# Keys of the last two batches transposed by DMA, their block sums added on GpSimd and VectorE, and u transposed from SBUF to SBUF

## The chip, the cores and the metric

The kernel runs on one NeuronCore of a Trainium2 chip, in one launch. The metric is the device time of one execution in microseconds (us). Three runs of the kernel before gave 272.8, 274.03 and 274.05 us; the median is 274.03. A further execution was taken with the hardware profiler: it took 272.19 us, of which 270.40 us are the span that the profile shows, from the first instruction to the last.

In the profile PE is TensorE (PEld its weight loads), DVE is VectorE, ACT is ScalarE, POOL is GpSimd and SP is SyncE. SPq is the queue of DMA issues on SP. L359 is line 359 of the kernel before.

## The reference

The input is q, k and v of shape (4 batches, 8 heads, 768 positions, 64). First comes a block-sparse attention, then a two-layer mixer on its output x of shape (4, 768, 512):

```python
k_rep = k.reshape(B, H, 12, 64, D).mean(axis=3)          # one mean key per block of 64
gate_scores = einsum('bhsd,bhnd->bhsn', q, k_rep)        # blocks of the future: -1e9
sel = top-3 blocks of gate_scores, and the own block     # per query
scores = q @ k.T / 8, where the block is selected and j <= i, else -1e9
attn_out = softmax(scores) @ v
...
xt = x.transpose(0, 2, 1)
h = maximum(xt @ w_tok1, 0) @ w_tok2
u = x + h.transpose(0, 2, 1)
out = u + maximum(u @ w_ch1, 0) @ w_ch2
```

So each head needs K transposed (for the scores) and the sums of K over blocks of 64 (for the gate), and each batch needs u and u transposed (for `u @ w_ch1`).

## The kernel before

The attention works on 16 pairs of heads, four to a batch. For a pair, the two heads lie side by side: K and Q are loaded as fp32 tiles of 128 positions by 6 blocks by 128 columns (`load_qk`, L265, two DMAs each, with rows of 256 bytes). TensorE transposes them in six 128x128 fp32 steps (`transposes`, L359) into PSUM; ScalarE copies the result to SBUF (`evac_t`, L368, tiles kt and qt); GpSimd casts it to fp16, one cast for each head, into KA and Q (`cast`, L374). VectorE sums kt over blocks (`ksum`, L382) and puts the sums in place (`kcopy`, L390). Then come the gate (five fp32 matmuls, L400), the top three on VectorE, a mask that is transposed on TensorE (L443) and copied into spare rows of Q (L451), the scores (three groups a head, L465), the exponentials on ScalarE (L478), the causal cut on VectorE (L485), the product with V (21 matmuls a head, L496), and the division by the row sums, which writes x16 (L515). V is loaded by one DMA a pair and cast on GpSimd (`cast_v`, L280).

For each batch the token mixer (`tok1` L527 and `umix` L539; for batch 0 in column parts, L558 and L572) gives u in fp16, 128 positions by 6 blocks by 512 columns (L547, L581). In batch 0, TensorE transposes u (L589) and VectorE copies it to uT (L597). In batches 1 to 3, SP stores u to DRAM (`store_u`, L344) and a DMA transpose reads it back into uT (`turn_u`, L350). The channel mixer is `ch1` (L608; for each of 12 groups of 128 hidden columns, 4 matmuls over 512 positions and 4 over 256), a ReLU on ScalarE (L618) or VectorE (L620), `ch2` (L629, 12 matmuls a block of 128 positions), an addition of u on VectorE (L637) and the output's store on SP (L641).

Nothing is ordered at run time. Every step is an `Op` with an engine, a cost in nanoseconds that its author wrote down, its dependences and a priority; `plan` places them one by one and gives each engine a fixed order, in which the instructions are then issued. An engine that waits for one instruction holds all that stand behind it. The pairs follow each other; the mixers of a finished batch fill the gaps. Tiles come from rings of fixed size (`RINGS`): two PSUM tiles `big` for scores and transposes, three PSUM banks, two kt tiles, three output tiles ob, and so on. A tile is handed out again once its last user is done.

The code holds a second way for K, for the pairs i >= VIA; with VIA = 16 no pair takes it. There, `load_k8` (L290) loads K of both heads as 96 partitions by 2 heads by 8 positions by 64 columns, in the ring of kt; `cast_k8` (L311) casts it into K16, a tile whose other columns hold zeros (`k16_zero`, L325) and block indicators (`k16_ind`, L329); `store_k` (L318) writes K16 to DRAM and `turn_k` (L322) transposes it by DMA from DRAM straight into KA; `ksum8` (L298) sums the 8 positions of each partition and `ksum_pe` (L305), one fp32 matmul with a 96x12 indicator, sums partitions to blocks.

Of the kernel before, what the change touches and what calls it, by code (L numbers as in the profile page):

```python
# [10 lines left out]
F16 = mybir.dt.float16  # L11
AF = mybir.ActivationFunctionType
ALU = mybir.AluOpType
AX = mybir.AxisListType
# [15 lines left out]
FIRST = 4  # L30
TRI = 1
EARLY = 1
VIA = 16
UVIA = 1
LEAD = 960.0
WARM, COLD, WARM_END = 120, 20, 17000.0
# [141 lines left out]
def kernel(  # L178
# [11 lines left out]
    nc = tc.nc  # L190
    B, H, S, D = q.shape
    NB = S // 64
    NJ = S // 128
    DM = H * D
    DT = moe_w_tok1.shape[1]
    DC = moe_w_ch1.shape[1]
    NCC = DM // 128
# [7 lines left out]
    dram = ctx.enter_context(tc.tile_pool(name="dr", bufs=1, space=bass.MemoryType.DRAM))  # L205
# [11 lines left out]
    def sb(tag, shape, dt, name):  # L217
        return sp.tile(shape, dt, tag=tag, bufs=RINGS[tag], name=name)

    def ps(tag, shape, name, dt=FP):  # L220
        if tag == "big":
            return pp.tile([128, 1024], FP, tag=tag, bufs=RINGS[tag], name=name)
        return pp.tile(shape, dt, tag=tag, bufs=RINGS[tag], name=name)
# [16 lines left out]
    T = {}  # L240
    ops = []

    def op(eng, occ, rec, deps, prio, fn, takes=(), size=0):
        o = Op(eng, occ, rec, deps, prio, fn, takes, size)
        ops.append(o)
        return o

    def pe(occ, deps, prio, fn, takes=(), tail=170):
        return op("PE", occ, occ + tail, deps, prio, fn, takes)
# [4 lines left out]
    def dve(occ, deps, prio, fn, takes=()):  # L254
        return op("DVE", occ, occ + 84, deps, prio, fn, takes)
# [12 lines left out]
    def load_v(i):  # L268
        b, h = pairs[i]

        def f():
            t = sb("v32", [128, 2, NJ, D], FP, f"v32_{i}")
            T["v32", i] = t
            nc.sync.dma_start(out=t.rearrange("p g j d -> p (g j) d"),
                              in_=v[b, h:h + 2].rearrange("g (j p) d -> p (g j) d", p=128))
        return f
# [7 lines left out]
    def load_k8(i):  # L284
        b, h = pairs[i]

        def f():
            t = sb("kt", [128, 2, 8, D], FP, f"k8_{i}")[0:96]
            T["k8", i] = t
            nc.sync.dma_start(out=t.rearrange("p g t d -> p g (t d)"),  # L290
                              in_=k[b, h:h + 2].rearrange("g (p t) d -> p g (t d)", t=8))
        return f

    def ksum8(i):
        def f():
            t = sp.tile([96, 2, D], FP, tag="kp", bufs=2, name=f"kp_{i}")
            T["kp", i] = t
            nc.vector.tensor_reduce(out=t, in_=T["k8", i].rearrange("p g t d -> p g d t"), axis=AX.X, op=ALU.add)  # L298
        return f

    def ksum_pe(i):
        def f():
            p = ps("bank", [128, NB], "kps")
            T["kst", i] = p
            nc.tensor.matmul(out=p, lhsT=T["kp", i].rearrange("p g d -> p (g d)"), rhs=blk, start=True, stop=True)  # L305
        return f

    def cast_k8(i):
        def f():
            y = i % 2  # L310
            nc.gpsimd.tensor_copy(out=K16[y].rearrange("p t (g c) -> p g t c", g=4)[:, 0:4:3, :, :], in_=T["k8", i])  # L311
        return f

    def store_k(i):
        def f():
            t = dram.tile([S, 256], F16, tag=f"ks{i % 2}", name=f"kscr_{i}")
            T["kscr", i] = t
            nc.sync.dma_start(out=t.rearrange("(p t) c -> p (t c)", t=8), in_=K16[i % 2].rearrange("p t c -> p (t c)"))  # L318
        return f

    def turn_k(i):
        return lambda: nc.sync.dma_start_transpose(out=KAX[:, i % R, :, :], in_=T["kscr", i])  # L322

    def k16_zero(y):
        return lambda: nc.gpsimd.memset(K16[y].bitcast(FP), 0.0)  # L325

    def k16_ind(y):
        def f():
            for c in (64, 128):  # L329
                nc.gpsimd.tensor_copy(out=K16[y][:, :, c:c + NB],  # L330
                                      in_=blk.rearrange("p (o n) -> p o n", o=1).broadcast_to([96, 8, NB]))
        return f

    def zero_q(r):
        def f():
            nc.gpsimd.memset(QA[r][0][64:128, :].bitcast(FP), 0.0)
            nc.gpsimd.memset(QA[r][1][0:64, :].bitcast(FP), 0.0)
        return f

    def store_u(b):  # L340
        def f():
            t = dram.tile([S, DM], F16, tag=f"us{b % 2}", name=f"uscr_{b}")
            T["uscr", b] = t
            nc.sync.dma_start(out=t.rearrange("(j p) c -> p j c", p=128), in_=T["u", b])  # L344
        return f

    def turn_u(b):
        def f():
            T["uT", b] = sb("uT", [128, NCC, S], F16, f"uT_{b}")
            nc.sync.dma_start_transpose(out=T["uT", b], in_=T["uscr", b])  # L350
        return f

    def transposes(t32, i):
# [31 lines left out]
    def kcopy(i):  # L385
        def f():
            kst = T["kst", i]
            r = i % R
            for lo, c in ((64, 0), (0, NB)):
                nc.vector.tensor_reduce(out=ks2[r][lo:lo + 64, c:c + NB],  # L390
                                        in_=kst[lo:lo + 64, :].rearrange("p (n o) -> p n o", o=1),
                                        axis=AX.X, op=ALU.add)
        return f
# [199 lines left out]
    def uput(b, cc):  # L593
        def f():
            if cc == 0:
                T["uT", b] = sb("uT", [128, NCC, S], F16, f"uT_{b}")
            nc.vector.tensor_copy(out=T["uT", b][:, cc, :], in_=T["utps", b, cc])  # L597
        return f

    CH = ((0, 512), (512, 768))  # L600
# [1 line left out]
    def ch1(b, fc, n):  # L602
        def f():
            a, e = CH[n]
            p = ps("bank", [128, e - a], "c1")
            T["c1", b, fc, n] = p
            for cc in range(NCC):
                nc.tensor.matmul(out=p, lhsT=wc1_16[:, cc, 128 * fc:128 * fc + 128],  # L608
                                 rhs=T["uT", b][:, cc, a:e], start=(cc == 0), stop=(cc == NCC - 1))
        return f  # L610

    def relu2(b, fc, n):
# [38 lines left out]
    O = {}  # L651
# [16 lines left out]
    for i in range(NP):  # L668
        b, h = pairs[i]
        base = 10.0 * i  # L670
        pre = 10.0 * (i - (AHEAD if i < FIRST else LATER))
        old = i - R

        def last_scores(x):
            return [O.get(("sc", old, x, g)) for g in range(3)]

        if i >= VIA:
            kb = Buf("kt")
            ld = op("SP", 500, 0, [], pre - 12, load_k8(i), [kb], size=1400)
            O["ksum", i] = dve(1100, [ld], pre + 1, ksum8(i))  # L680
            nb = Buf("bank")
            O["kpe", i] = pe(115, [O["ksum", i]], pre + 1, ksum_pe(i), [nb])
            O["kcopy", i] = dve(260, [O["kpe", i], O.get(("gate", old))], pre + 1, kcopy(i))
            nb.users.append(O["kcopy", i])
            y = i % 2
            if i < VIA + 2:
                O["kz", y] = op("POOL", 1100, 1150, [], pre - 1, k16_zero(y))
                O["ki", y] = op("POOL", 400, 450, [O["kz", y]], pre - 1, k16_ind(y))
            O["castk", i] = op("POOL", 1150, 1200, [ld, O["ki", y], O.get(("kst", i - 2))], pre + 3, cast_k8(i))
            kb.users += [O["ksum", i], O["castk", i]]  # L690
            O["kst", i] = op("SPO", 600, 0, [O["castk", i], O.get(("cast", "kt", i, 0))], pre + 3.1, store_k(i), size=1600)
            O["kturn", i] = op("SPO", 600, 0, [O["kst", i]] + last_scores(0) + last_scores(1), pre + 3.2, turn_k(i), size=2500)
            O["cast", "kt", i, 0] = O["cast", "kt", i, 1] = O["kturn", i]
        zq = [op("POOL", 880, 930, [], pre - 1, zero_q(i))] if 0 < i < R else []
        for t32, src, off in (("kl", k, 0), ("ql", q, 0.1))[i >= VIA:]:
            bf = Buf(t32)
# [4 lines left out]
            name = "kt" if t32 == "kl" else "qt"  # L701
            tb = Buf(name)
# [19 lines left out]
        ld = op("SP", 500, 0, [], pre + 2, load_v(i), [vb], size=1700)  # L722
# [47 lines left out]
    for b in range(B):  # L770
        fill = 1000.0 * (b + 1)
        mix = fill - LEAD if b else fill
        early = -1.0
        norms = [O["norm", i, x] for i in range(4 * b, 4 * b + 4) for x in range(2)]
        hb = Buf("h1")
        ub = Buf("u")
        if b == 0:
# [13 lines left out]
            uadds = [[O["uadd", b, c, n] for n in range(2)] for c in range(4)]  # L791
        else:
# [12 lines left out]
            uadds = [[O["uadd", b, j] for j in range(NJ)]] * NCC  # L805
        tb = Buf("uT")
        if b >= UVIA:
            O["ust", b] = op("SPO", 600, 0, uadds[0], early, store_u(b), size=3000)
            O["uturn", b] = op("SPO", 600, 0, [O["ust", b]], early, turn_u(b), [tb], size=3500)
            ub.users.append(O["ust", b])  # L810
        for cc in range(NCC if b < UVIA else 0):
            bk = Buf("bank")
            O["utr", b, cc] = pe(336, uadds[cc], mix + (cc + 0.6 if b == 0 else 10 + cc), utr(b, cc), [bk])
# [16 lines left out]
        for j in range(NJ):  # L830
            cuts = ((0, DM),) if b < B - 1 or j < NJ - 1 else ((0, 320), (320, DM))
            for lo, hi in cuts:
# [11 lines left out]
                s = op("SPO", 600, 0, [o], early, store(b, j, lo, hi), size=2 * (hi - lo))  # L844
# [76 lines left out]
```

## Time and profile before

| | |
|---|---|
| median of three runs | 274.03 us |
| profiled execution | 272.19 us, span 270.40 |
| six K transposes of a pair on PE, L359 | 96 instructions in all 16 pairs |
| evacuation of K on ACT, L368 | 16, 799 ns each |
| casts of K on POOL, L374 | 32, 845 ns each |
| sums of K on DVE, L382 | 15 of 942 ns and one of 957 |
| weight loads issued on POOL, L663 and L665 | 8, 384 KB each |
| store of u, L344, issue to landing | 3.7 to 7.7 us |
| DMA transpose of u, L350 | three, 3.5 to 4.3 us on SPq, 5.6 to 7.7 to landing |

A group of the profile shows the line, the engine, the operation, what it writes and reads, the shapes, the count, then the busy time, the mean of one in ns, and the idle time of the engine before it with what ended it. The time of one matmul includes its latency; matmuls overlap, so what one costs is read from the start of one to the start of the next. The slices cut the span into 40 parts of 6.76 us; a digit is the busy share in tenths.

### The profile page before, as it was taken

To read this page: it belongs to the slowest core of one execution; us is meant where nothing else is said; L and a number is where in the kernel's file an instruction comes from. 1 tells how busy PE (TensorE), PEld (TensorE's weight loads), DVE (VectorE), ACT (ScalarE), POOL (GpSimd) and SP (SyncE) were. 2 spreads that over 40 slices of the span, in tenths; PEclk is the share of its full clock that TensorE was granted. 3 is DMA by queue.
4 is the path that set the end of the run, shared out by engine and by line. 5 is a ranking of instruction groups with operands and counts; after the bars stand their busy time and mean duration, and the time that the engine had idled before them with its cause. 6 is when DMAs were issued, how large, how long until landed. Compare 5 with 4: busy or idle time off the path is not lost.

```text
span 270.4 us, 5927 instructions
## 1 busy us (share of the span) xinstructions
PE 262.6 (97%) x2309; PEld 174.5 (65%) x2309; DVE 161.0 (60%) x561; ACT 142.6 (53%) x188; POOL 81.5 (30%) x112
## 2 busy tenths in 40 slices
PE   8899999999999999999999999999999999999994
PEld 5787588877787877776876655544455544465443
DVE  4558968997979777879888533334233252333222
ACT  2367997777888898788487704430024400044100
POOL 8688816763465365336432000000000000000000
PEclk9999999999999999999999999999999999999999
DMA  8999999999999985480741121003920017510032
GB/s 173 205 212 224 189 215 214 197 200 200 213 209 228 212 176 133 103 174 3 158 117 41 39 77 42 0 2 116 260 89 2 0 48 196 153 72 0 2 135 97
DMA packets 94411, 34.67 MB, mean 128 GB/s; under 512 B 85616, under 2 KB 90888, under 8 KB 94384
## 3 DMA queue, kind: packets, MB, share of 16 engines
q1 hardware_dynamic: 90272, 29.89, 50.5%
q0 software_dynamic: 3392, 4.15, 9.1%
q8 instruction: 18, 0.29, 0.5%
q10 hardware_dynamic: 720, 0.25, 0.5%
q14 instruction: 9, 0.07, 0.1%
HBM read 27.21 MB, written 8.65 MB: 133 GB/s over the span
## 4 chain that ended last, share of the span: by engine, by line
PE 87%; DMA 4%; DVE 4%; ACT 3%; issue 1%; SPq 1%; DVEq 0%; ACTq 0%
PE c L629 23%; PE c L608 23%; PE sps L465 12%; PE aps L496 7%; PE gps L400 5%; DMA ql<-in_q_dram 4%; PE tql L359 4%; PE ups L539 3%; PE tkl L359 3%; PE tok L527 3%; ACT e L478 3%; PE bps L443 2%; PE warm L648 1%; PE tok L558 1%; DVE Q L451 1%
## 5 line engine op out<-in xcount | busy, mean ns | idle before, releaser
L478 ACT ACTIVATE e<-sps 128x1024 f16<-128x1024 f32 (+1 forms) x96 | 84.6, 918 | 16.9 <-PE sps L465 12.0
L608 PE MATMUL c<-uT,wc 128*128 128x256 f16 (+1 forms) x384 | 68.1, 326 | 0.2 <-ACT h L618 0.2
L618 ACT ACTIVATE h<-c 128x512 f16<-128x512 f32 x48 | 28.7, 598 | 69.0 <-PE c L608 61.7
L629 PE MATMUL c<-wc,h 128*128 128x512 f16 (+2 forms) x300 | 64.9, 370 | 0.0
L608 PEld LDWEIGHTS <-wc 128*128 128x128 f16 x384 | 37.1, 98 | 24.5 <-issue 0.4
L465 PE MATMUL sps<-Q,KA 128*128 128x512 f16 (+3 forms) x256 | 50.1, 305 | 1.0 <-ACT e L478 0.7
L629 PEld LDWEIGHTS <-h 128*128 128x128 f16 x300 | 28.8, 98 | 31.3 <-issue 0.6
L620 DVE TENSOR_SCALAR h<-c 128x256 f16<-128x256 f32 x48 | 20.2, 420 | 33.8 <-PE c L608 33.8
L637 DVE TENSOR_TENSOR ob<-u,c 128x512 f32<-128x512 f16 (+2 forms) x25 | 16.6, 666 | 38.4 <-PE c L629 38.4
L485 DVE TENSOR_TENSOR e<-e,m 128x256 f16<-128x256 f16 x90 | 31.1, 353 | 12.9 <-ACT e L478 12.2
L374 POOL CAST KA<-kt 64x768 f16<-64x768 f32 x32 | 27.0, 845 | 27.4 <-ACT kt L368 24.2
L465 PEld LDWEIGHTS <-KA 128*128 128x128 f16 x256 | 22.4, 100 | 15.2 <-issue 1.2
L374 POOL CAST Q<-qt 64x768 f16<-64x768 f32 x32 | 26.9, 841 | 10.8 <-ACT qt L368 9.3
L496 PE MATMUL aps<-V,e 128*128 128x65 f16 x672 | 27.0, 193 | 0.1
L496 PEld LDWEIGHTS <-e 128*128 128x128 f16 x672 | 25.6, 98 | 2.2 <-issue 0.4
L400 PEld LDWEIGHTS gps<-ks,qt 128*128 128x128 f32 x160 | 19.2, 192 | 2.4 <-DVE ks L390 1.3
L280 POOL CAST V<-v 128x768 f16<-128x768 f32 x16 | 13.3, 832 | 24.0 <-DMA v<-in_v_dram 19.8
L400 PE MATMUL gps<-ks,qt 128*128 128x24 f32 x160 | 20.0, 267 | 0.3 <-DVE ks L390 0.2
L368 ACT COPY kt<-tkl 128x768 f32<-128x768 f32 x16 | 12.8, 799 | 11.7 <-PE tkl L359 5.9
L515 DVE TENSOR_TENSOR x<-aps,rc 128x384 f16<-128x384 f32 x32 | 17.6, 550 | 0.5
L451 DVE COPY Q<-bps 12x640 f16<-12x640 f16 x32 | 15.5, 484 | 1.9 <-PE bps L443 0.8
L368 ACT COPY qt<-tql 128x768 f32<-128x768 f32 x16 | 12.8, 798 | 6.5 <-PE tql L359 5.7
(55 smaller groups left out, 218.0 us busy)
## 6 DMA issues: line engine op xcount, KB each, us to landing
kl<-in_k_dram SPq DMA_DIRECT2D x32, 192.0 KB, 4.8
ql<-in_q_dram SPq DMA_DIRECT2D x32, 192.0 KB, 4.6
v<-in_v_dram SPq DMA_DIRECT2D x16, 384.0 KB, 5.4
out_dram<-ob SPq DMA_DIRECT2D x23, 256.0 KB, 2.0
wc<-in_moe_w_ch_dram POOLq DMA_DIRECT2D x8, 384.0 KB, 7.4
uscr<-u SPq DMA_DIRECT2D x3, 768.0 KB, 3.7
w<-in_moe_w_tok_dram POOLq DMA_DIRECT2D x2, 384.0 KB, 6.8
out_dram<-ob SPq DMA_DIRECT2D x1, 160.0 KB, 1.8
```

Of the source, the lines that this page charges most:

```text
L359: nc.tensor.transpose(out=p[:, 128 * j:128 * j + 128], in_=t[:, j, :], identity=ident32)
L368: nc.scalar.copy(out=t, in_=p[:, 0:S])
L374: nc.gpsimd.tensor_copy(out=dst[i % R][x][lo:lo + 64, :], in_=T[name, i][lo:lo + 64, :])
L400: nc.tensor.matmul(out=g[:, j, :], lhsT=T["qt", i][:, 128 * j + 128:128 * j + 256], rhs=ks2[i % R], start=True, stop=True)
L465: nc.tensor.matmul(out=p[:, off + a:off + a + n], lhsT=KA[i % R][x][:, 128 * kk:128 * kk + 128], rhs=QA[i % R][x][:, q0 + a:q0 + a + n], s ...
L478: nc.scalar.activation(out=e[:, 0:width], in_=T["sps", i, x, g][:, 0:width], func=AF.Exp, scale=scale)
L485: nc.vector.tensor_tensor(out=d, in0=d, in1=m0, op=ALU.mult)
L496: nc.tensor.matmul(out=p[:, jq, :], lhsT=T["e", i, x, g][:, o:o + 128], rhs=V16[i % (R + 1)][:, x, kk, :], start=(kk == 0), stop=(kk == jq))
L608: nc.tensor.matmul(out=p, lhsT=wc1_16[:, cc, 128 * fc:128 * fc + 128], rhs=T["uT", b][:, cc, a:e], start=(cc == 0), stop=(cc == NCC - 1))
L618: nc.scalar.activation(out=T["h2", b][:, fc, a:e], in_=T["c1", b, fc, n], func=AF.Relu)
L620: nc.vector.tensor_scalar(out=T["h2", b][:, fc, a:e], in0=T["c1", b, fc, n], scalar1=0.0, scalar2=None, op0=ALU.max)
L629: nc.tensor.matmul(out=T["c2", b, j, lo], lhsT=T["h2", b][:, fc, 128 * j:128 * j + 128], rhs=wc2_16[:, fc, lo:hi], start=(fc == 0), stop=( ...
```

## The change

`VIA` goes from 16 to 8, so that pairs 8 to 15 (batches 2 and 3) take the second way for K. In that way the sums are made differently: the reduction over 8 positions becomes one fp32 addition on GpSimd, in place, of positions 4 to 7 onto 0 to 3 (`ksum4`, 512 elements a partition), and two on VectorE (256 and 128 elements). The cast is planned ahead of the addition, and the clearing of K16 comes after the casts of Q of pairs 5 and 6. `store_u` goes; `turn_u` reads u from SBUF and writes uT in blocks, so that uT is 6 position blocks by 4 column blocks by 128 (read by `ch1` through a rearranged view). Costs that the planner works with change with it.

```diff
-VIA = 16
+VIA = 8
...
+    def ksum4(i):
+        def f():
+            p = T["k8", i]
+            nc.gpsimd.tensor_tensor(out=p[:, :, 0:4, :], in0=p[:, :, 0:4, :], in1=p[:, :, 4:8, :], op=ALU.add)
+        return f
...
-            nc.vector.tensor_reduce(out=t, in_=T["k8", i].rearrange("p g t d -> p g d t"), axis=AX.X, op=ALU.add)
+            p = T["k8", i]
+            nc.vector.tensor_tensor(out=p[:, :, 0:2, :], in0=p[:, :, 0:2, :], in1=p[:, :, 2:4, :], op=ALU.add)
+            nc.vector.tensor_tensor(out=t, in0=p[:, :, 0, :], in1=p[:, :, 1, :], op=ALU.add)
...
-    def store_u(b):
...
-            T["uT", b] = sb("uT", [128, NCC, S], F16, f"uT_{b}")
-            nc.sync.dma_start_transpose(out=T["uT", b], in_=T["uscr", b])
+            t = sb("uT", [128, NJ, NCC, 128], F16, f"uT_{b}")
+            T["uT", b] = t.rearrange("p j c s -> p c j s")
+            nc.sync.dma_start_transpose(out=t.rearrange("p j c s -> p (j c) s"), in_=T["u", b].rearrange("p j c -> p (j c)"))
...
-                                 rhs=T["uT", b][:, cc, a:e], start=(cc == 0), stop=(cc == NCC - 1))
+                                 rhs=T["uT", b][:, cc, a // 128:e // 128, :], start=(cc == 0), stop=(cc == NCC - 1))
...
-            O["ksum", i] = dve(1100, [ld], pre + 1, ksum8(i))
+            y = i % 2
+            if i < VIA + 2:
+                O["kz", y] = op("POOL", 1000, 1050, [O["cast", "qt", 5 + y, 1]], pre - 1, k16_zero(y))
+                O["ki", y] = op("POOL", 400, 450, [O["kz", y]], pre - 1, k16_ind(y))
+            O["castk", i] = op("POOL", 1000, 1040, [ld, O["ki", y], O.get(("kst", i - 2))], pre + 3, cast_k8(i))
+            O["ksum4", i] = op("POOL", 1150, 1200, [O["castk", i]], pre + 1, ksum4(i))
+            O["ksum", i] = dve(560, [O["ksum4", i]], pre + 1, ksum8(i))
+            kb.users += [O["ksum", i]]
...
-            O["ust", b] = op("SPO", 600, 0, uadds[0], early, store_u(b), size=3000)
-            O["uturn", b] = op("SPO", 600, 0, [O["ust", b]], early, turn_u(b), [tb], size=3500)
-            ub.users.append(O["ust", b])
+            O["uturn", b] = op("SPO", 2500, 0, uadds[0], early, turn_u(b), [tb], size=3500)
+            ub.users.append(O["uturn", b])
```

More of the change, by code (lines that the diff above doesn't have):

```diff
@@ L338, in zero_q @@
         return f
-    def store_u(b):
[L341 to L345, printed above, removed]
     def turn_u(b):
         def f():
-            T["uT", b] = sb("uT", [128, NCC, S], F16, f"uT_{b}")
-            nc.sync.dma_start_transpose(out=T["uT", b], in_=T["uscr", b])
+            t = sb("uT", [128, NJ, NCC, 128], F16, f"uT_{b}")
+            T["uT", b] = t.rearrange("p j c s -> p c j s")
+            nc.sync.dma_start_transpose(out=t.rearrange("p j c s -> p (j c) s"), in_=T["u", b].rearrange("p j c -> p (j c)"))
         return f
@@ L595, in f @@
             if cc == 0:
-                T["uT", b] = sb("uT", [128, NCC, S], F16, f"uT_{b}")
-            nc.vector.tensor_copy(out=T["uT", b][:, cc, :], in_=T["utps", b, cc])
+                T["uT", b] = sb("uT", [128, NCC, NJ, 128], F16, f"uT_{b}")
+            nc.vector.tensor_copy(out=T["uT", b][:, cc].rearrange("p j s -> p (j s)"), in_=T["utps", b, cc])
         return f
@@ L684 @@
             nb.users.append(O["kcopy", i])
[L685 to L690, printed above, removed]
             O["kst", i] = op("SPO", 600, 0, [O["castk", i], O.get(("cast", "kt", i, 0))], pre + 3.1, store_k(i), size=1600)
```

## The prediction

> **What bounds the kernel now.** I read the page's busy times and slices first, then the chain of work that ended last, then the stages in which the changed code runs.
>
> ```profile
> PE 262.6 (97%) x2309; PEld 174.5 (65%) x2309; DVE 161.0 (60%) x561; ACT 142.6 (53%) x188; POOL 81.5 (30%) x112
> PE   8899999999999999999999999999999999999994
> DMA  8999999999999985480741121003920017510032
> PE 87%; DMA 4%; DVE 4%; ACT 3%; issue 1%; SPq 1%; DVEq 0%; ACTq 0%
> ```
>
> TensorE is the bound: 97% of the span, 87% of the chain, and no thin slice until the last. The DMA engines are full as well, but only for the first 14 slices (to 95 us). Busy time by stage confirms it for the stage where pairs 8 to 15 are prepared (columns: length, then busy us and instructions of PE, PEld, DVE, ACT, POOL, clock, DMA share, GB/s):
>
> ```profile
> 80.00:100.00 20.00, 20.00 (x231) 15.60 (x231) 16.40 (x69) 17.78 (x24) 10.59 (x14) 1.00 1.14 217
> 120.00:160.00 40.00, 40.00 (x420) 27.65 (x419) 31.20 (x114) 26.63 (x32) 11.97 (x14) 1.00 0.31 75
> ```
>
> PE has no idle time there. So a matmul removed is time saved, one for one, and a wait added to PE's fixed order is time lost, one for one, since no later idle time gives it back.
>
> [...] 18 warm-up matmuls at the start took 4.02 us, 223 ns each, and later ones 109 ns each (11 in 1.36 us, the last with its latency).
>
> ```profile
> 1.07 4.02 PE L648 MATMUL warm<-warm 128*128 128x256 f16 x18 [1.07 <-DVE warm L852]
> 8.47 1.36 PE L648 MATMUL warm<-warm 128*128 128x256 f16 x11
> ```
>
> **Part 1: K work on PE, eight pairs.** Removed: 6 fp32 transposes a pair. Their mean of 279 ns is latency; in the chain in order of time six take 0.66 us. Added: one fp32 matmul a pair (block sums). Nearest row: the gate, five fp32 matmuls with the same 128-column weight load in 1.08 us, 0.22 us each.
>
> ```profile
> L359 PE MATMUL tkl<-id,kl 128*128 128x128 f32 x96 | 13.6, 279 | 0.2 <-issue 0.2
> 83.80 0.67 PE tkl L359 x6
> 106.36 1.08 PE gps L400 x10
> ```
>
> Sum: 8 x 0.66 - 8 x 0.22 = 3.5 us saved, all on the path. ACT loses 8 evacuations (0.80 each, 6.4 us) and DVE 8 reductions of 942 ns against 16 adds of 256 and 128 elements (between the rows 128x120 fp32, 278 ns, and 128x512, 676 ns: about 0.42 + 0.29 = 0.71 a pair), 1.9 us less. Neither engine is the bound (17.8 and 16.4 of 20 us), so this is worth nothing by itself.
>
> **Part 2: GpSimd.** Removed: 16 casts x 0.845 = 13.5 us. Added: 8 casts of 1024 elements (832 ns for 768, so 1.1), 8 adds of 1.25, two clears of 1024 (412 ns for 384, so about 1.0) and four small copies (about 0.2): 8.8 + 10 + 2 + 0.8 = 21.6. GpSimd is busy half the time at 80 to 100 us, so the 8 us extra fit. What does not fit is one instruction that the diff doesn't show: built, the changed program has a reload of GpSimd's instruction library directly ahead of its first tensor_tensor, the add of pair 8. It sits in the middle of the program, behind a cast that waits for a load. Its place in time, from these lines of before (GpSimd, then landings of a V load issued at 54.3 and of the K halves issued from 57.4):
>
> ```profile
> 60.97 1.51 POOL L665 DMA_DIRECT2D wc<-in_moe_w_ch_dram  x2
> 64.35 0.83 POOL L280 CAST V<-v 128x768 f16<-128x768 f32 x1 [1.88 <-DMA v<-in_v_dram]
> 74.33 0.92 POOL L280 CAST V<-v 128x768 f16<-128x768 f32 x1 [2.93 <-DMA v<-in_v_dram]
> v<-in_v_dram SPq DMA_DIRECT2D x1, 384.0 KB, 9.9
> kl<-in_k_dram SPq DMA_DIRECT2D x2, 192.0 KB, 8.3
> ```
>
> Up to pair 6's V load SP's order is unchanged, so that V lands at 64.3 again. K of pair 8 is next in the queue, where the two K halves landed at 65.8 to 68.3; I take 67.2. Supply: cast 67.2 to 68.3, reload L, add 1.25, two DVE adds with their hand-over 0.85, so the block-sum matmul of pair 8 may start at 70.4 + L. Demand: PE's order in the changed program starts the channel MLP of batch 0 where it could before (59.96, held by the uT copy of L597), then runs up to that matmul: six 512-column groups x 0.86, five 256-column groups x 0.43, five scores groups of pair 5 (1.83), two aV (1.33), transposes of K 7 (0.66), 11.1 us in all: 71.1. Slack 0.7 us; the rest of L is idle PE. DVE's queue, too, stands behind the add, and kt of pair 6, whose buffer slot the K tile of pair 8 holds until its sums are made; both wait for what PE waits for already.
>
> L: from below, 0 [...]; from above 10, because the DMA engines are full here and a load that must cross them took 9.9 us to land where others in this kernel took 4.3. I take 7. Idle: 7 - 0.7 = 6.3 us. [...] Part 2 costs 6.3 + 1.7 = 8.0 us.
>
> Afterwards GpSimd's queue holds V 7, casts of K 6, cast of K 9, casts of Q 7, add of K 9: 0.83 + 1.71 + 1.1 + 1.71 + 1.25 = 6.6, plus 0.85, 7.45 us after the first add ends (76.55 at L = 7): 84.0. PE wants pair 9's sums 7.7 us after pair 8's (77.4 + 7.7 = 85.1): no second wait. With L = 0 the V load that lands at 74.3 would hold that queue, supply 81.8 against demand 78.9 and cost up to 2.9; so even a free reload leaves -0.6 to -3.5.
>
> **Part 3: K through DRAM.** A pair has two K loads of 256-byte rows less, and one load of 2 KB rows, one store and one transpose more. SP waits for the cast before each store and for the landed store before each transpose; behind stand loads of Q and V for later pairs and, near the end, output stores. Nearest row: uT, 768x512, 3.5 to 4.3 us on SP's queue and 5.6 to 7.7 to landing; K is half. Tightest is pair 8: store of pair 9 at about 80.3 (its cast), transpose behind it, landed by 88.4 even at 7.7 us; PE wants these scores 8.1 us after pair 9's sums, 93.2. Nothing is on the path: 0, at worst 2 us. If that cover went, each late transpose would cost its delay once.
>
> **Part 4: u turned from SBUF.** The store of u (3.7 to 4.6 us to landing) goes. In batch 3 it was hidden:
>
> ```profile
> 221.21 0.38 SPq L344 DMA_DIRECT2D uscr<-u  x1
> 226.57 3.53 SPq L350 DMA_TRANSPOSE uT<-uscr  x1
> 220.04 15.70 PE L629 MATMUL c<-wc,h 128*128 128x512 f16 x72
> 235.58 15.76 PE L608 MATMUL c<-uT,wc 128*128 128x512 f16 x96
> ```
>
> The turn ended near 232.2 (5.6 after issue) and its reader starts at 235.6 behind the channel MLP of batch 2. Gain 0. A transpose from SBUF is in no trace; it may take up to 14 us from 221 before it shows, twice the slowest one seen. Output stores now stand behind it on SP: with three output buffers and two outputs every 5.2 us that stands 6 us. So 0, above that up to 3 us in each of batches 2 and 3. uT is read in runs of 128 columns: no row shows such a read; 0, at worst 2 us.
>
> **Sum.** -3.5 + 8.0 + 0 + 0 = +4.5. Against the profiled execution (272.19 us: span 270.40 and 1.79 around it) 276.7. The median of the runs shown is 274.03, 1.84 above that execution; I add the change to it: 278.5.
>
> **Rivals.** *The reload is short* (0.20): PE never waits for it beyond 3 us, and the removed transposes decide: -3.5, with the late V load -0.6; about 271.8 (270.5 to 273.4). For it: no trace here shows a load, and it may be nearly free. Against: slack of 0.7 us. It decides while L is under 4.2. *Draw* (0.11): L of 4 to 6 without the clock drop, within 0.5% of 274.03. *A DMA wait besides* (0.07): SBUF transposes or K's way through DRAM come late, on top of the reload, about 285. For it: operations never seen; against: margins of 5 and more us.
>
> **Numbers.** Forecast (reload stalls PE): 0.62, own range 275.5 to 283 [...]. Range for 8 in 10: 271 to 283, from most of the short reload up to the longest stall; the bound for a difference that can be told is 0.5%, 1.4 us. Faster 0.19, same 0.12, slower 0.69.
>
> **What would show it.** A gap on PE of 5 to 9 us near 71 us, ahead of a 128x12 fp32 matmul, with GpSimd silent between a 96x1024 cast and its first tensor_tensor; PE clock below 1 after it; from there PE full and K transposes of eight pairs gone. Wrong: no such gap (then about 271), GpSimd's gap under 4 us, or PE idle ahead of scores (L465) or the channel MLP (L608) of batches 1 to 3.

## The result, and the profile after

The changed kernel took 284.35 us, the median of four runs (282.42 to 286.68), against 273.49 for the kernel before on the same chip: a ratio of 1.0375, interval [1.031, 1.0439]. The change costs about 10 us. I had forecast 278.5 and a range of 271 to 283. The size was wrong; the sign came out right by luck, since the wait that I had named, a long reload of GpSimd's library, isn't in the trace at all.

Executions of some of these versions fall into two groups that differ in how long TensorE runs at half clock; every ratio is of the faster group, while the profiles of e6 and e10 were taken in the slower one, so that the long half clock seen in them (about 13.6 us in each) is in their spans and not in their ratios.

The page of the changed kernel, busy times, slices and chain (its profiled execution took 284.52 us, span 282.7):

```profile
PE 262.3 (93%) x2277; PEld 172.0 (61%) x2277; DVE 170.3 (60%) x569; ACT 136.9 (48%) x180; POOL 89.8 (32%) x118
PE   7799999989679879999988999999999999999994
DVE  5468868965589999889698576325133262233222
PEclk9999999999999799999999999999999999999999
DMA  8999999899999779989981312000921007120032
PE 60%; DVE 16%; DMA 14%; issue 3%; POOL 3%; ACT 2%; SPq 1%; DVEq 0%; POOLq 0%
```

PE's busy time is what it was (262.6 before), but the span is 12.3 us longer, so PE now waits for 20.4 us instead of 7.8. The thin slices of PE lie between 56 and 156 us (slices of 7.07 us), where its row was full. In the chain PE falls from 87% to 60%; VectorE rises from 4% to 16%, and the DMA engines from 4% to 14%, over half of that loads of V. Most of PE's listed waits now end with VectorE. VectorE's own busy time grew by 9.3 us, where I had reckoned 1.9 less.

The stage in which the pairs of the new way are prepared and worked on, first of the kernel before, then of the changed one (columns: length, then busy us and instructions of PE, PEld, DVE, ACT, POOL, clock, DMA share, GB/s):

```profile
60.00:160.00 100.00, 99.76 (x1075) 72.68 (x1074) 80.35 (x312) 77.94 (x97) 40.74 (x50) 1.00 0.69 141
```

```profile
60.00:160.00 100.00, 88.81 (x907) 62.77 (x904) 80.16 (x286) 63.65 (x79) 46.92 (x53) 0.98 0.98 195
```

Here PE is idle for 11.2 us against 0.24. That is 11.0 of the 12.6 us by which PE's waits grew, so the experiments below are compared in this stage.

**The wait for the reload is not there.** GpSimd's timeline around its first addition:

```profile
71.02 1.04 POOL L319 CAST K<-k 96x1024 f16<-96x1024 f32 x1 [1.14 <-DMA k<-in_k_dram]
72.14 1.25 POOL L297 TENSOR_TENSOR k<-k 96x512 f32<-96x512 f32 x1
```

The cast ends at 72.06 and the addition starts at 72.14. I had put a reload of 7 us between them, which was my own estimate: no trace of before holds one. The trace here has no line of a reload, and leaves at most 0.08 us for it between the two. PE's gap ahead of pair 8's sums is 2.38 us (it starts them at 74.22). The loads of V and K make it: GpSimd waited 5.85 us for that V and began its cast at 69.05, where I had put 64.3, and the cast of K followed at 71.02 instead of 67.2.

**What VectorE does instead.** The groups of VectorE that grew or are new in the changed kernel, and L410 for comparison (busy us and mean ns of one, then idle time before it):

```profile
L434 DVE SCALAR_TENSOR_TENSOR bn<-lt,own 128x120 f16<-128x120 f32 x16 | 7.3, 456 | 0.2
L426 DVE TENSOR_TENSOR lt<-gm,m 128x120 f32<-128x120 f32 x16 | 7.3, 455 | 0.3
L305 DVE TENSOR_TENSOR k<-k 96x256 f32<-96x256 f32 x8 | 4.5, 560 | 2.9 <-POOL k L297 2.9
L306 DVE TENSOR_TENSOR kp<-k 96x128 f32<-96x128 f32 x8 | 4.5, 560 | 0.3
L410 DVE TENSOR_TENSOR gm<-gps,gbias 128x120 f32<-128x120 f32 x16 | 4.4, 277 | 6.9 <-PE gps L402 6.9
```

The two steps lt and bn, by which the top three become a mask (lt compares with the third maximum, bn makes the mask's bias of that), are the same code on the same shapes as before, where each took 278 ns. A mean of 456 hides two kinds. By line, the least, median and longest of bn before (L432) and in the changed kernel (L434) are:

```profile
L432 DVE SCALAR_TENSOR_TENSOR bn<-lt,own x16: 244/282/284, 12.4 to 146.6; 128x120 f16<-128x120 f32 x16
L434 DVE SCALAR_TENSOR_TENSOR bn<-lt,own x16: 238/280/1998, 12.5 to 164.5; 128x120 f16<-128x120 f32 x16
PEld L445: 5.4, 6
PE bps L445: 3.7, 4
```

Most are untouched, and some last up to seven times as long; TensorE's mask transposes (L445, the two lower lines: who waited for bn, us and times) then stand still. L410 did not change (its longest is 283 ns): it has the same shape as L426, but one of its inputs lies in PSUM. The long ones are those with both inputs in SBUF: the longest of L426, L434, L487, L305 and L306 are 1155, 1998, 1375, 1255 and 1237 ns, while no other group of VectorE's has one more than 20 ns above the median of its shape. When they end is the clue. GpSimd and then VectorE in the changed kernel, over the same 6 us:

```profile
86.62 1.85 POOL L376 CAST Q<-qt 64x768 f16<-64x768 f32 x2
88.53 1.04 POOL L319 CAST K<-k 96x1024 f16<-96x1024 f32 x1
90.36 1.40 POOL L297 TENSOR_TENSOR k<-k 96x512 f32<-96x512 f32 x1
```

```profile
87.70 0.90 DVE L434 SCALAR_TENSOR_TENSOR bn<-lt,own 128x120 f16<-128x120 f32 x1
88.72 0.99 DVE L487 TENSOR_TENSOR e<-e,m 128x256 f16<-128x256 f16 x1
90.74 1.16 DVE L426 TENSOR_TENSOR lt<-gm,m 128x120 f32<-128x120 f32 x1
```

Add start and duration: GpSimd's instructions end at 88.47, 89.57 and 91.76, VectorE's at 88.60, 89.71 and 91.90, each 0.13 to 0.14 us later. Each of these VectorE instructions seems to wait until GpSimd has finished the instruction in hand. The longest waited through a second one: the bn of 1998 ns runs from 144.35 to 146.35 us, past the end of an addition (145.44), and ends 0.14 us after the cast of V that follows it at once (146.21). The traces show three things: these four long instructions end 0.13 to 0.14 us after one of GpSimd's, while most keep their time (median of bn 280 ns, before 282); only those with two SBUF inputs are long; and with memsets in place of GpSimd's reads (e6 below) bn takes at most 286 ns.

Why didn't the kernel before suffer, whose GpSimd was busy for 81.5 us, most of them casts that read? GpSimd and VectorE in the kernel before:

```profile
80.29 1.77 POOL L374 CAST Q<-qt 64x768 f16<-64x768 f32 x2
87.60 1.71 POOL L374 CAST Q<-qt 64x768 f16<-64x768 f32 x2
```

```profile
82.50 0.27 DVE L424 TENSOR_TENSOR lt<-gm,m 128x120 f32<-128x120 f32 x1
91.26 0.27 DVE L424 TENSOR_TENSOR lt<-gm,m 128x120 f32<-128x120 f32 x1
```

The casts of Q are over (82.06, 89.31) before the top three reach lt. In the changed kernel the K cast and the addition stand there, and push other casts into that time too. The kernel before was not spared altogether: of its causal cuts (L485, two SBUF inputs too), whose median is 284 ns, the longest took 953; but no wait of PE for them is listed.

My theory P: GpSimd's reads hold up VectorE's two-input instructions on the way from the gate to the mask and to the block sums, and PE waits. Rivals: T, the order of the work (the K tiles share the ring of kt, so pair 6 stands behind pairs 8 and 9); C, the sums as a longer chain with late loads; U, the transposes of u from SBUF.

### The profile page after: what moved, and what is told of

It is laid out like the page before. It is cut to its first block, busy times and chain, and to the rows that moved or that the text cites. A ratio compares the mean times of both kernels' runs of the same rounds, so it can differ in the third digit from the quotient of the medians.

```text
span 282.7 us, 5873 instructions
## 1 busy us (share of the span) xinstructions
PE 262.3 (93%) x2277; PEld 172.0 (61%) x2277; DVE 170.3 (60%) x569; ACT 136.9 (48%) x180; POOL 89.8 (32%) x118
## 4 chain that ended last, share of the span: by engine, by line
PE 60%; DVE 16%; DMA 14%; issue 3%; POOL 3%; ACT 2%; SPq 1%; DVEq 0%; POOLq 0%
PE c L631 21%; PE c L610 18%; DMA v<-in_v_dram 8%; PE sps L467 5%; PE aps L498 4%; DMA ql<-in_q_dram 4%; DVE e L487 3%; PE gps L402 2%; DVE m L419 2%; PE ups L541 2%; DMA w<-in_moe_w_tok_dram 2%; PE tql L361 2%; PE tok L529 2%; DVE bn L434 2%; DVE kp L306 1%
## 5 line engine op out<-in xcount | busy, mean ns | idle before, releaser
L610 PE MATMUL c<-uT,wc 128*128 128x256 f16 (+1 forms) x384 | 66.9, 326 | 0.0
L487 DVE TENSOR_TENSOR e<-e,m 128x256 f16<-128x256 f16 x90 | 31.6, 357 | 10.3 <-ACT e L480 9.5
L467 PEld LDWEIGHTS <-KA 128*128 128x128 f16 x256 | 23.0, 101 | 15.9 <-issue 0.9
L498 PE MATMUL aps<-V,e 128*128 128x65 f16 x672 | 28.1, 194 | 2.3 <-DVE e L487 1.8
L498 PEld LDWEIGHTS <-e 128*128 128x128 f16 x672 | 26.0, 98 | 5.8 <-DVE e L487 3.0
L376 POOL CAST KA<-kt 64x768 f16<-64x768 f32 x16 | 13.2, 828 | 13.3 <-ACT kt L370 12.7
L361 PE MATMUL tql<-id,ql 128*128 128x128 f32 x96 | 13.8, 283 | 1.7 <-DMA ql<-in_q_dram 1.7
```

Of the source, the lines that this page charges most:

```text
L361: nc.tensor.transpose(out=p[:, 128 * j:128 * j + 128], in_=t[:, j, :], identity=ident32)
L376: nc.gpsimd.tensor_copy(out=dst[i % R][x][lo:lo + 64, :], in_=T[name, i][lo:lo + 64, :])
L467: nc.tensor.matmul(out=p[:, off + a:off + a + n], lhsT=KA[i % R][x][:, 128 * kk:128 * kk + 128], rhs=QA[i % R][x][:, q0 + a:q0 + a + n], s ...
L487: nc.vector.tensor_tensor(out=d, in0=d, in1=m0, op=ALU.mult)
L498: nc.tensor.matmul(out=p[:, jq, :], lhsT=T["e", i, x, g][:, o:o + 128], rhs=V16[i % (R + 1)][:, x, kk, :], start=(kk == 0), stop=(kk == jq))
```

## The experiments

**e1, u alone.** The changed kernel with no pair on the new way.

```diff
-VIA = 8
+VIA = 16
```

> The u part alone: no pair takes the DMA way for K, u is transposed from SBUF. Both theories of the loss (P: VectorE instructions with two SBUF inputs are held up by GpSimd and VectorE then holds PE; C: the longer chain to the sums of K has no slack in PE's fixed order) say the u part costs nothing: within 0.5% of the kernel before, transpose 5.6 to 6.1 us to landing, PE never waiting for uT. A rival, U (the SBUF transpose and the outputs behind it on SP cost part of the loss), says 2 us slower or more.

Measured: 273.35 us, ratio 1.0008 [0.998, 1.0036]. Turning u from SBUF neither costs nor gains.

**e2, K alone.** The changed kernel with `store_u` and the transpose of u from DRAM put back.

```diff
-            nc.sync.dma_start_transpose(out=t.rearrange("p j c s -> p (j c) s"), in_=T["u", b].rearrange("p j c -> p (j c)"))
+            nc.sync.dma_start_transpose(out=T["uT", b], in_=T["uscr", b])
...
```

> The K part alone: pairs 8 to 15 by DMA, u stored and read back as before. P and C: as slow as the changed kernel, ratio to before 1.03 to 1.045. U: clearly less, ratio under 1.025.

Measured: 284.52, ratio 1.0399 [1.0346, 1.0452]. The whole loss is in the K part. This run also says something of rival C. Its profile has the loads of pair 8 on time (GpSimd's cast of K, then PE's block sums of pair 8):

```profile
65.42 1.04 POOL L319 CAST K<-k 96x1024 f16<-96x1024 f32 x1 [0.88 <-DMA k<-in_k_dram]
71.02 0.37 PE L313 MATMUL kps<-blk,kp 96*128 96x12 f32 x2
```

PE did not wait for these sums, and the loss is as large, so the 2.38 us of the changed kernel's profile are not what makes it. PE waited 2.63 us for the sums of pair 9 instead, whose addition stood behind a V that GpSimd had to wait for and behind casts of Q.

**e3, no addition on GpSimd, the same order.**

```diff
-            nc.gpsimd.tensor_tensor(out=p[:, :, 0:4, :], ...
+            pass
...
+            nc.vector.tensor_reduce(out=t, in_=T["k8", i].rearrange("p g t d -> p g d t"), axis=AX.X, op=ALU.add)
...
```

> The changed kernel in the same planned order, but the addition on GpSimd is left out and VectorE makes the sums of 8 positions in one reduction (one SBUF input) instead of two additions; the result is the same. GpSimd has 10 us less work, VectorE 16 instructions with two SBUF inputs fewer. P: instructions with two SBUF inputs on L426 and L434 come down from 456 ns towards 278, and PE's waits for the mask (bn, 3.7 us) and for the diagonal (e, 1.8 us) shrink with those for the sums; ratio to before about 1.015. C: only the waits for the sums (kp, 5.3 us) go, those for bn and e stay; ratio about 1.02 with L426 and L434 near 450.

Measured: 283.32, ratio 1.0364 [1.0316, 1.0413]. Both theories had expected less (1.015 and 1.02), and the run tells nothing apart, because the reduction cost far more than I had reckoned:

```profile
L303 DVE TENSOR_REDUCE kp<-k 96x128 f32<-96x1024 f32 x8 | 15.2, 1899 | 0.0
```

The hold-ups did shrink (bn 335 ns), but the sums took 15.2 us of VectorE instead of 9.0. What was taken off VectorE was put back.

**e4, a dose of reads in the kernel before.** K takes the old way; GpSimd gets three copies of scratch tiles after the Q casts of each pair from 6 on (30 copies, 32.5 us), which nobody waits for.

```diff
+            if i >= 6 and name == "qt" and x == 1:
+                for _ in range(3):
+                    nc.gpsimd.tensor_copy(out=K16[1][:, 0:4, :], in_=K16[0][:, 0:4, :])
...
```

> The kernel before with added GpSimd work that nobody needs: after the second cast of Q of each pair from 6 on, three copies of 1024 fp16 elements from SBUF to SBUF (scratch), about 30 us in 100. No chain to the sums of K is longer. P: VectorE's instructions with two SBUF inputs (278 ns on L424 and L432, 353 on L485) stretch by the wait for the copy in flight, means above 400 on L424 and L432, and the kernel gets slower by 1 to 5 us. C: they stay near 278 and the time is that of before within 0.5%, or slower only by PE waiting for casts.

Measured: 287.57, ratio 1.0544 [1.0487, 1.0601]. The groups of VectorE, then one of PE's gaps on its timeline:

```profile
L435 DVE SCALAR_TENSOR_TENSOR bn<-lt,own 128x120 f16<-128x120 f32 x16 | 10.2, 640 | 0.2
L427 DVE TENSOR_TENSOR lt<-gm,m 128x120 f32<-128x120 f32 x16 | 6.7, 418 | 0.2
```

```profile
118.08 0.45 PE L446 MATMUL bps<-id,bn 128*128 128x128 f16 x5 [1.58 <-DVE bn L435]
```

Copies that no step depends on reproduce the picture: bn and lt stretch, PE waits 7.6 us for bn and 1.6 for the causal cuts, and is idle for 10.2 us of the stage (89.83 busy). No wait of PE for a cast of GpSimd is listed, which C had left open. The loss of about 15 us is far above the 1 to 5 that P had expected: the direction was foreseen, the size was not. Copies on GpSimd alone are enough to cost 5%, whatever K does. It doesn't yet say that GpSimd's reads are what costs in the change.

**e5, a ring of its own for the K tiles**, GpSimd's work as in the change.

```diff
-                  x16=3, h1=2, u=2, uT=2, h2=1, ob=3)
+                  x16=2, k8=2, h1=2, u=2, uT=2, h2=1, ob=3)
...
-            kb = Buf("kt")
+            kb = Buf("k8")
```

> The changed kernel with the fp32 K tiles of pairs 8 to 15 in a ring of their own (two), no longer in the ring of kt; to make room, x16 has two buffers instead of three and kt tiles are 768 columns. The planner then keeps pair 6 and 7 ahead of pairs 8 and 9, as before, and spreads the channel MLP of batch 0 over the pairs. T (the order: the shared ring delays pair 6, PE spends its filler early, VectorE idles at 60 to 80 us and is crowded after): most of the loss goes, ratio to before 0.99 to 1.005, VectorE never above 18.5 busy in 20 us. P (GpSimd's instructions hold up VectorE's with two SBUF inputs, whatever the order): GpSimd's work is the same, ratio still 1.02 or more, the comparison with the third maximum and the bias that follows it still above 400 ns.

Measured: 282.37, ratio 1.0311 [1.0248, 1.0375]. 0.6 points come back, with the intervals overlapping: T is not the main cause. What the ring is worth by itself is not read cleanly here: in its profile PE waits 17.3 us instead of 20.4, but runs longer at half clock (mean clock 0.979 against 0.994).

**e6, GpSimd writes and doesn't read.** For pairs 8 to 15 the casts of Q, V and K and the addition become memsets, in the same order of work.

```diff
-            nc.gpsimd.tensor_tensor(out=p[:, :, 0:4, :], ...
+            for _ in range(2):
+                nc.gpsimd.memset(p[:, :, 0:4, :], 0.5)
...
```

> The changed kernel in the same planned order, with GpSimd as busy, but not reading SBUF: for pairs 8 to 15 its casts of Q, V and K and its addition are replaced by memsets of about their length, so Q, K and V of these pairs are constants and the output of batches 2 and 3 is not the reference's. P: the comparison and the bias come back to about 280 ns (from 455), PE's waits for bn and e (5.4 us) nearly go and those for the sums (5.3) shrink, ratio to before 1.00 to 1.02. T: the crowding stays, ratio 1.03 or more, though the two instructions are at 280 ns.

Measured: ratio 1.0014 [0.9985, 1.0044], lt 307 and bn 275 ns:

```profile
L442 DVE SCALAR_TENSOR_TENSOR bn<-lt,own x16: 243/276/286, 12.7 to 158.0; 128x120 f16<-128x120 f32 x16
```

GpSimd was as busy in the stage as the changed one, near enough (42.6 us against 46.9), in the same order, and the loss was gone. So it is the reading, more than GpSimd's load. One thing goes along with it: a memset no longer waits for what the cast had to read (the load of V or K, the evacuation of Q). e2, where the loads of pair 8 were on time, and e10 and e11 below, where nothing of this is left out, don't rest on that. A wait of 1.96 us for the sums of pair 9 is still there: that much is GpSimd's queue and a late V, and not the hold-ups.

**e7, four pairs only**, and **e8, the same with the ring of e5.**

```diff
-VIA = 8
+VIA = 12
...
-                O["kz", y] = op("POOL", 1000, 1050, [O["cast", "qt", 5 + y, 1]], pre - 1, k16_zero(y))
+                O["kz", y] = op("POOL", 1000, 1050, [O["cast", "qt", 9 + y, 1]], pre - 1, k16_zero(y))
```

> The DMA way for pairs 12 to 15 only (four pairs; K16 is cleared after the casts of Q of pairs 9 and 10). P and T: about half the loss or less, ratio 1.01 to 1.02, since the shared ring and GpSimd's work remain for four pairs; a saving of 1.8 us on PE is in it.

> As the run with pairs 12 to 15 only, with the K tiles in a ring of their own (and two x16 buffers, kt of 768 columns). T: no crowding, the removed transposes show: ratio 0.993 to 1.0. P: ratio 1.005 to 1.015.

Measured: 277.22, ratio 1.0147 [1.0068, 1.0227], and 277.9, 1.014 [1.0083, 1.0196]. Half of the pairs cost somewhat under half of the loss, and the ring makes no difference there.

**e9, only the added reads become writes** (cast of K and addition, as in e6; those of Q and V still read).

```diff
-            nc.gpsimd.tensor_copy(out=K16[y].rearrange(...)[:, 0:4:3, :, :], in_=T["k8", i])
+            nc.gpsimd.memset(K16[y].rearrange(...)[:, 0, :, :], 0.5)
+            nc.gpsimd.memset(K16[y].rearrange(...)[:, 3, :, :], 0.5)
...
```

> The changed kernel in its own order, with only GpSimd's added work changed: the cast of K and the add of the block sums become memsets that write and don't read (K16 and the tile of sums hold constants for batches 2 and 3, so that their output is not the reference's). The casts of Q and V stay as they are and still read. If the added reads themselves lock VectorE out: 273 to 276 us, ratio 1.00 to 1.01, the subtractions of the top three (lt, bn) near 300 ns. If it is the casts of Q and V, moved to a bad time by the added work ahead of them in GpSimd's queue: 280 to 283 us, lt and bn over 400 ns, since memsets of like length move them all the same. If the order of the work is the cause: 282 to 285.

Measured: 276.53, ratio 1.0091 [1.0045, 1.0138]. bn fell to 313 ns, lt to 381. So about three quarters of the loss (1.0375 to 1.0091) are reads that the change added; the casts of Q and V, moved into VectorE's way, are part of the rest (e6: 1.0014). The memsets differ from the cast in their waits here too.

**e10, nothing added on GpSimd**, and **e11, only the cast taken off it.** In both ScalarE casts K; in e10 VectorE makes the third addition as well.

```diff
-            nc.gpsimd.tensor_copy(out=K16[y].rearrange(...)[:, 0:4:3, :, :], in_=T["k8", i])
+            nc.scalar.copy(out=K16[y].rearrange(...)[:, 0:4:3, :, :], in_=T["k8", i])
...
-            nc.gpsimd.tensor_tensor(out=p[:, :, 0:4, :], ...
+            nc.vector.tensor_tensor(out=p[:, :, 0:4, :], ...
...
```

> The changed kernel with nothing added on GpSimd: the cast of K goes to ScalarE, which lost an evacuation for it, and the third addition of the block sums to VectorE (8 x about 0.7 us more there). Nothing of the computation is left out. If GpSimd's reads are the cause: lt and bn under 310 ns, and with 3.5 us of transposes gone from TensorE 270 to 273.5 us, ratio 0.985 to 1.00. If VectorE is late because it has too much to do with any sums by additions: 278 to 283. If the order or the late loads at 60 to 75 us are the cause: 281 to 285.

> The changed kernel with only the cast of K moved from GpSimd to ScalarE; GpSimd keeps the addition. Nothing of the computation is left out. If the reads are the cause, about half of the added reading is left (10.3 of 19.0 us): 276 to 280 us, ratio 1.01 to 1.02, lt and bn between 310 and 420 ns. If order or loads are the cause: 281 to 285.

Measured: e11 279.56, ratio 1.0192 [1.0122, 1.0263]; e10 ratio 1.0117 [1.0086, 1.0148]. Off GpSimd, the cast brings back 1.8 points, in keeping with P, and the addition about 0.8 more, with overlapping intervals. But e10 missed what P expected: the ratio (0.985 to 1.00), and lt and bn, which took 371 and 388 ns instead of under 310; GpSimd still casts Q and V, and K of the other pairs. Three lines of e10's trace, ScalarE's and PE's timelines and one stretch after them, say what else was left:

```profile
76.41 1.04 ACT L319 CAST K<-k 96x1024 f16<-96x1024 f32 x1 [2.39 <-DMA k<-in_k_dram]
78.20 1.54 PE L361 MATMUL tql<-id,ql 128*128 128x128 f32 x6 [1.84 <-ACT qt L370]
```

```profile
80.00:84.00 4.00, 4.00 (x21) 3.81 (x22) 3.42 (x15) 2.09 (x3) 3.55 (x6) 0.50 1.31 230
```

PE waits 1.84 us for an evacuation of Q, which on ScalarE stands behind the cast of K of pair 9, and that cast waited 2.39 us for its load. Within that gap the clock falls to half; in this execution that lasted from 77.6 to 91.2 us and cost 7 us (mean clock 0.975), which the ratio does not hold. The wait is in theory T's place (the shared ring sets the order) and in C's (full DMA engines, first pairs late), so both had to be asked again without the added reads.

**e12, e10 for four pairs** (the edit of e7 on e10), and **e13, e10 with a ring of its own** (the edit of e5 on e10).

```diff
-                  x16=3, h1=2, u=2, uT=2, h2=1, ob=3)
+                  x16=2, k8=2, h1=2, u=2, uT=2, h2=1, ob=3)
```

> Pairs 12 to 15 alone take K by DMA, with the cast on ScalarE and all three additions on VectorE, so nothing is added on GpSimd; u is turned from SBUF. Nothing of the computation is left out. Half of the transposes go: 4 x (0.66 - 0.22) = 1.8 us of TensorE. If what is left of the loss in the version with eight pairs (1.2%) comes from the crowded stage at 60 to 100 us, where the DMA engines are full and the first pairs of the new way come late: 270.5 to 273 us, ratio 0.99 to 1.00. If it comes from the additions on VectorE or from the way through DRAM in any stage: 274 to 276, ratio 1.005.

> The version with the cast on ScalarE and the additions on VectorE for eight pairs, with a ring of its own for the K tiles (two k8, two x16 instead of three, kt as small as before), so that pair 6 need not wait for the K tiles of pairs 8 and 9. Nothing of the computation is left out. If the remaining loss is the shared ring's order (TensorE waited 1.84 us near 78 us for an evacuation and then ran 10 us at half clock): 270 to 273 us, ratio 0.985 to 1.00, clock above 0.99. If it is the load on VectorE or on the DMA engines: 275 to 279 as without the ring.

Measured: e12 273.3, ratio 0.9983 [0.9961, 1.0005]; e13 274.44, ratio 1.0019 [0.9995, 1.0043]. The stage in e13:

```profile
60.00:160.00 100.00, 97.29 (x1022) 68.61 (x1020) 84.41 (x326) 76.19 (x96) 33.14 (x39) 1.00 0.99 197
```

With the added reads and the shared ring both gone, PE idles 2.7 us in the stage instead of 11.2, and the time is that of the kernel before; the cast of K of pair 9 starts at 77.80 there, without a wait. e12 came out as expected if the crowded stage is the rest of the loss. e13 just missed both of its ranges (0.985 to 1.00, or 275 us and more), nearer to the ring's. The ring that was worth 0.6 points under the reads (e5), with overlapping intervals, is worth 1.0 (1.0117 to 1.0019) without the added ones. Neither version is faster than the kernel before by more than the measurement tells.

## Why the prediction was wrong

PE busy time between 60 and 160 us in the profiled execution, with its clock, beside the ratio:

| version | PE busy of 100 us | clock | ratio |
|---|---|---|---|
| before | 99.76 | 1.00 | 1 |
| changed | 88.81 | 0.98 | 1.0375 |
| e11: K cast on ScalarE | 94.67 | 0.98 | 1.0192 |
| e10: addition on VectorE too | 96.71 | 0.93 | 1.0117 |
| e13: a ring of its own too | 97.29 | 1.00 | 1.0019 |

At half clock PE is busy longer with the same work (six transposes of Q in the changed kernel: 1.48 us at 93.97, at half clock, and 0.82 at 81.17, at full clock), so e10's 96.71 holds less work than its neighbours' figures (934 matmuls of the stage, 954 in e11 and 1022 in e13); its ratio is the figure to compare.

- **Part 2, the reload (8.0 us): failed.** Nothing of it shows: 0.08 us lie between the cast and the addition. Its 7 us were my estimate, and so were the 1.7 us for a half clock behind its gap; no trace of before showed a reload, or a clock that drops behind a gap. I never asked whether anything else could stop VectorE. "What would show it" had named the refutation, a gap on GpSimd under 4 us; the time it gave for that case, about 271, was wrong by 13 us. One part of that case held: its wait at pair 9's sums, up to 2.9 us, was 2.63 in e2 and 1.96 in e6.
- **Part 1, "Neither engine is the bound", and Part 2, "the 8 us extra fit": these are the steps that failed.** I compared busy shares, and so put what GpSimd's reads do to VectorE at nothing. With no reload the working left a change of -0.6 to -3.5 us; the measured one is about +10, and it is mostly this term that is missing. VectorE's work depends on what GpSimd does at the same moment: lt and bn took 5.6 us more between them (7.3 less 4.5 each), the additions 9.0 us instead of 5.7. VectorE, counted 1.9 us lighter, came out 9.3 us heavier, and it stands between the gate and the mask, where PE's fixed order has nothing else to do. Of PE's waits in the changed kernel, the listed ones for VectorE sum to 11.7 us: 5.3 at the sums (L313), 3.7 at the mask (L445), 1.8 at the product with V (L498), 0.9 at u; of the 5.3, 2.38 are the late loads of pair 8.
- **PE's saving of 3.5 us: in part seen, and spent.** In e10, PE's 266.1 us less the 7 of half clock are 259.1, 3.5 below the 262.6 of before; in e9, at full clock, PE is busy for 259.7, 2.9 below. But in e13, at full clock too, it is 262.0, only 0.6 below. In the changed kernel half clock (3.4 us long) took 1.7 back, and the waits more than the rest.
- **Clock.** I had tied a drop to the reload's gap of 6.3 us, and that too was only my estimate. The clock dropped without such a gap: after gaps of 0.65 and 0.95 us at 90 to 93 us in the changed kernel (1.00 up to 93, then 0.58 over the next us and 0.50 over the two that follow), and in one of 1.84 in e10. A single gap's length doesn't decide it: the 2.38 us ahead of pair 8's sums brought no drop (1.00 from 70 to 80 us). What sets it is not shown by these runs.
- **GpSimd's durations: right.** Addition 1285 ns (1.25 forecast, my estimate, since no trace of before has such an addition), cast of K 1082 (1.1), clears 952 (1.0).
- **Part 3, K through DRAM: right as far as PE's waits show.** Store 6.0 and transpose 5.6 us to landing (medians), and no wait of PE for KA is listed. Not foreseen was the shared ring with the late loads; without the added reads it is worth about 1% (e10 against e13).
- **Part 4, u from SBUF: right.** e1: ratio 1.0008.
- **Open:** e13 should be 3.5 us faster than the kernel before, and isn't. In its profile PE is idle for 2.5 us more in the stage, mostly in waits for VectorE, whose sums are additions of 0.67, 0.59 and 0.54 us a pair there. Ahead of the stage PE waits 1.5 us for a load of the token mixer's weights (L560), of which the profile of before lists nothing. And PE's busy time is only 0.6 us less; why not 3.5, I can't place. Nor is it fully shown how much of the changed kernel's loss falls to late loads: what is left at pair 9's sums once reads become writes, 1.96 us in e6 and 2.03 in e9, is the nearest figure.

## What to carry to other kernels

Before giving GpSimd work that reads SBUF, list what VectorE runs at that time with two SBUF inputs, and which engine waits for it: GpSimd's free time was not free here (32.5 us of copies that nobody waits for cost 5% in e4). In these traces a hold-up lasted for what was left of GpSimd's instruction (ends 0.13 to 0.14 us apart), in the longest case with the whole of the next one (1998 ns instead of 278). Read a group's least, median and longest time, not its mean, and compare the ends of two engines' instructions. A freed share of the bound engine is worth something only if the engines that feed it stay on time: here 3.5 us of PE's work were to go, and the kernel lost about 10.

## What the hardware did that I had not expected

- A VectorE instruction of 278 ns with two inputs in SBUF took up to 2.0 us (bn, longest), ending 0.13 to 0.14 us after GpSimd's. The longest waited through two of GpSimd's instructions in a row (1998 ns in the changed kernel). With memsets on GpSimd in place of the reads this was not seen (e6: bn at most 286).
- A GpSimd library reload in mid-program: no line of it in the trace, and at most 0.08 us between the cast and the addition where I had placed it (changed kernel).
- A VectorE reduction over a strided innermost dimension: 1899 ns for 96x1024 fp32 (e3), against 942 for 128x768 contiguous: 1.85 ns an element against 1.23. No run separates the stride from the other differences.
- A DMA transpose of 768x512 fp16 from SBUF landed 5.9 us after its issue (5.6 to 7.7 from DRAM).
- Half clock on TensorE for 3.4 us (changed kernel) to about 13.6 us (e6, e10), in or after single gaps of no more than 2 us (0.65 and 0.95 in the changed kernel, 1.96 in e6, 1.84 in e10), where one of 2.38 brought none.
